# Loading q with its token blocks outermost in a fused attention and feed-forward kernel

## The chip, the cores and the metric

The kernel runs on one core of a Trainium2 chip. Its time is the device time of one execution in microseconds (us). The kernel before took 860.06 us in the median of three runs (860.0 to 861.02). Five engines work side by side, each through its own fixed list of instructions: TensorE (PE; its weight loads are shown apart as PEld), VectorE (DVE), ScalarE (ACT), GpSimd (POOL) and SyncE (SP), whose list here is nearly all DMA issues. The transfers themselves are carried out by 16 DMA engines.

## The reference

Three stages follow each other; shapes are q, k, v (4, 8, 576, 64) and phi (4, 8, 576, 32), all float32.

```python
a = exp(phi - max(phi, axis=2)); a = a / (sum(a, axis=2) + 1e-09)      # over the 576 tokens
k_m = einsum('bhsm,bhsd->bhmd', a, k); v_m = einsum('bhsm,bhsd->bhmd', a, v)   # 32 memory slots per head
scores = (q @ k_m^T) / sqrt(64); attn = softmax(scores, axis=-1)
x = (attn @ v_m) laid out as (4 * 576 tokens, 8 heads * 64)            # 2304 x 512
x = (h * sigmoid(h)) @ w_out,  h = x @ w_in                            # 512 -> 2048 -> 512
out = ((x @ w_a) * (x @ w_b)) @ w_out2                                 # 512 -> 1536 -> 512
```

## The kernel before

The program has three parts. The first one, some 125 us long, loads q, k, v, phi and the first weights and computes the attention of the four batches b = 0 to 3, and begins the first feed-forward stage on the batches that are ready. The second and third parts, the rest of the time, are the two feed-forward stages; they hold no work on q.

In the first part each batch goes through these steps. `weights(b)` (line 629) turns phi into exponentials on VectorE and ScalarE (tiles `m`, `mxa`, `mb`, `ex`). `memory(b)` (line 656) forms k_m and v_m on TensorE (tile `kvp`), scales them (`kvn`) and turns k_m (`kt`, `kT`); `values(b)` turns v_m (`vt`). `turn(b, hg, n)` (line 720) turns q. The eight heads are taken in two groups, hg = 0 and 1, with four heads x = 0 to 3 each. A tile `qq` holds one group of one batch: 128 partitions, each with J * D = 18 * 64 numbers, which is the stretch of 18 neighbouring tokens of one head; 32 such blocks i make up a head's 576 tokens. TensorE transposes 128 columns at a time (two tokens of 64 numbers) into a PSUM tile `qt`, three transposes for each n = 0, 1, 2; ScalarE copies `qt` to the tile `qT` in SBUF (line 731). A column of `qT` is a partition of `qq`. `scores(b, hg, p)` (line 751) takes 32 columns per head from `qT` (line 768), so the head is expected as the outer and the block as the inner index of a column. The softmax of the scores (tiles `x`, `mxq`, `smq`, `xt`, `at`) follows on VectorE and ScalarE. `vw_first` multiplies v_m into the weights (`mp`, `m0h`, `m0l`), and `mul_h` and `mul_y` are the feed-forward products (`hp`, `yp`).

All loads are issued by SP in one written order (`LOADS`, line 955): phi of b = 1 and 0, a piece of w_out, q of (b 0, hg 0), w_out, w_in, k and v of b = 0, two pieces of w_in, q of (0, 1), k and v of b = 1, q of (1, 1), w_out, q of (1, 0), (2, 0), (2, 1), phi of b = 2 and 3, w_in, k and v of b = 2, k and v of b = 3, w_out, q of (3, 0), (3, 1). An issue waits until the buffer that it fills is free: there are two for `qq`, two pairs for k and v, three staging tiles for weights. SP also keeps at most eight loads open: each load uses one of eight completion counters in turn and waits until the load that used it before has landed. The order of the instructions of every engine is set ahead of time by a planner (`run`, line 566) with fixed assumed durations (1500 ns for a load of q, 490 ns for a copy of `qt`); on the chip each engine runs its list in that order whatever the real durations are. The planner also puts products of a tile of ones (`ones`) between TensorE's instructions where it expects a wait.

Of the kernel before, what the change touches and what calls it, by code (L numbers as in the profile page):

```python
# [13 lines left out]
AF = mybir.ActivationFunctionType  # L14
# [6 lines left out]
def attn_moe_moe2_kernel(  # L21
# [59 lines left out]
    V, A, GP, T, Y = (Pinned(e) for e in (nc.vector, nc.scalar, nc.gpsimd, nc.tensor, nc.sync))  # L81
# [444 lines left out]
    def op(eng, ns, after=(), done=None, take=None, free=(), wait=100, table=None, rec=0):  # L526
        takes = [] if take is None else [take] if isinstance(take[0], str) else list(take)
        return eng, ns, after, done, takes, free, wait, table, rec
# [78 lines left out]
    def bank_of(kind, name):  # L607

        pool, tag = {"bank": (ps_t, "t"), "hp": (ff["h"], "hp"), "yp": (ff["y"], "yp")}[kind]
        ps = pool.tile([128, W], F32, tag=tag, name=name)  # L610
        keep_busy(ps)
        return ps
# [107 lines left out]
    def turn(b, hg, n):  # L720

        t = st[b]
        yield op("T", 650, [f"q{b}{hg}"] + [f"qT{b}{hg}"] * (n > 0), done=f"qT{b}{hg}" if n == 0 else None,
                 take=[(BANK_Q[b], f"qt{b}{hg}{n}")] + [("qT", f"qT{b}{hg}")] * (n == 0), rec=6)
        if n == 0:
            t["qT", hg] = p_s.tile([128, J // 2, 128], F32, tag="qT", bufs=2, name="qT")
        qt = bank_of(BANK_Q[b], "qt")[:, :384].rearrange("p (i s) -> p i s", i=3)
        for i in range(3):
            T.transpose(qt[:, i], t["qq", hg][:, 128 * (3 * n + i) : 128 * (3 * n + i) + 128], ident)
        yield op("A", 490, done=f"qt{b}{hg}{n}", free=[f"qt{b}{hg}{n}"] + [f"qq{b}{hg}"] * (n == 2))  # L730
        A.activation(out=t["qT", hg][:, 3 * n : 3 * n + 3], in_=qt, func=AF.Copy)

    def low_half(way, v_ns, a_ns, hi, lo, src, done, free):

# [108 lines left out]
    def loads():  # L843

        st["w"] = {}
        for what in LOADS:
            kind, b, hg = what[:-2].rstrip("0123456789"), int(what[-2]), int(what[-1])
            if kind == "phi":
                yield op("D", 1500, done=f"phi{b}", take=("ph", f"ph{b}"))
                ph = st[b]["ph"] = p_in.tile([128, 4, JP, NM], F32, tag="ph", name="ph")  # L850
                Y.dma_start(
                    out=ph.rearrange("p x c m -> p x (c m)"),
                    in_=phi[b].rearrange("(x r) (p c) m -> (r p) x (c m)", r=2, p=64),
                )
            elif kind == "kv":
                yield op("D", 3050, done=f"kv{b}{hg}", take=("kv", f"kv{b}{hg}"))
                kv = st[b]["kv", hg] = p_in.tile([128, 2, 2, JP * D], F32, tag="kv", name="kv")
                for i, s in enumerate((k, v)):
                    src = s[b, 4 * hg : 4 * hg + 4].rearrange("(x r) (p c) d -> (r p) x (c d)", r=2, p=64)
                    Y.dma_start(out=kv[:, i], in_=src)  # L860
            elif kind == "q":

                yield op("D", 1500, done=f"q{b}{hg}", take=("qq", f"qq{b}{hg}"))
                qq = st[b]["qq", hg] = p_in.tile([128, J * D], F32, tag="qq", bufs=2, name="qq")
                src = q[b].rearrange("(x g) (i j) d -> g x i (j d)", g=2, i=32)[hg]
                Y.dma_start(out=qq, in_=src)
            else:
                c = hg
                name = f"{kind}{c}"
                yield op("D", 1400, done=f"load_{name}", take=("st", f"st_{name}"))  # L870
                s64 = st["w"][name] = p_w.tile([128, W], U64, tag="st", bufs=3, name="st_" + name)
                if kind == "wi":

                    r0, c0 = 256 * (c % 2), 256 * (c // 2)
                    src = w_in[r0 : r0 + 256, c0 : c0 + 256].rearrange("(a p) n -> p a n", p=128)
                    Y.dma_start(out=s64.rearrange("p (a b) -> p a b", a=2), in_=src)
                else:
                    Y.dma_start(out=s64, in_=w_out[c * 128 : c * 128 + 128, :])
# [95 lines left out]
    free_at["T"] = 5400.0  # L974
    free_at["D"] = 1900.0
    add(0, loads())
    add(R["units"][0], feed_forward())
    for b in range(B):
        add(R["weights"][b], weights(b))
        add(R["memory"][b], memory(b))  # L980
        if SUMS[b] == "V":
            add(R["sums"][b], sums(b))
        add(R["values"][b], values(b))
        for hg in range(2):
            for n in range(3):
                add(R[f"turn{hg}"][b], turn(b, hg, n))
            for p in range(len(parts_of(b))):
                add(R[f"scores{hg}" if p == 0 else f"late{hg}"][b], scores(b, hg, p))
        if b == 0:
            add(R["first"][0], vw_first(0, (0,)))  # L990
            add(R["vw"][0], vw_first(0, (1,)))
        else:
            add(R["vw"][b], vw_first(b, (0, 1)))
# [39 lines left out]
    with ExitStack() as mctx:  # L1033
# [110 lines left out]
        def due_weights(n):  # L1144
            return 10 + (START + NP * NS * QUARTER * (n // WG) - 8000.0 - 22000.0 * (WG - 1 - n % WG)) / 1000
# [173 lines left out]
        for n in later:  # L1319
            t = due_weights(n)  # L1320
# [36 lines left out]
```

## Time and profile before

| what | value |
|---|---|
| median of three runs | 860.06 us (860.0 to 861.02) |
| the profiled execution, whole | 860.02 us |
| its span, first to last instruction | 858.2 us |
| PE busy in the span | 808.8 us, 94% |
| PE busy in the first 125 us | 82.23 us |
| PE busy from 125 to 160 us | 35.00 us of 35 |
| eight loads of q | 576 KB each, 128 pieces of 4608 bytes |

A row of the chain of waits names what the work that ended last was waiting for. A row of the timeline gives the start, the length, the engine, the operation with output and inputs, the number of instructions that it merges, and in brackets how long the engine had been idle and what ended that wait. In the windows, PEclk is the granted TensorE clock as a share of the full 2.4 GHz (0.50 is 1.2 GHz), and the DMA share is the mean busy share of the 16 DMA engines.

### The profile page before, as it was taken

The page shows a single profiled execution, that of the slowest core. Times are in us where ns is not written, and L with a number is a line of the kernel's source. Part 1 is how long each engine was busy: PE and PEld are TensorE (multiplying, and loading weights), DVE is VectorE, ACT ScalarE, POOL GpSimd, SP SyncE. Part 2 cuts the span into 40 slices and gives each one's busy share as a digit, 9 for nine tenths or more (in the row PEclk, how much of TensorE's full clock was granted, in tenths as well). Part 3 has the DMA queues.
Part 4 walks back from the last instruction along what each step waited for, and adds up shares of the span by engine and source line. Part 5 has one row for each costly group of instructions (what it writes and reads, how often), then busy time and mean ns, then how long its engine had stood idle before and what let it go on. Part 6 is the DMA issues. An engine that isn't in the chain of part 4 may idle for free.

```text
span 858.2 us, 14574 instructions
## 1 busy us (share of the span) xinstructions
PE 808.8 (94%) x5826; PEld 744.7 (87%) x5826; DVE 536.6 (63%) x1052; ACT 440.7 (51%) x891; POOL 56.9 (7%) x71
## 2 busy tenths in 40 slices
PE   4664889999999999999999999999999999999997
PEld 3453779979999999999989999999999999999996
DVE  3564678765664666666579887486764865634534
ACT  1534577876565446566646766635443553322220
POOL 0000000000000000022200111101010110100000
PEclk8778989999999999999999999999999999999999
DMA  9828620253222123254466969979775985656753
GB/s 236 224 101 212 197 77 1 75 146 76 75 62 62 50 75 99 43 121 102 87 242 249 289 193 284 286 227 278 223 215 185 274 241 169 185 179 202 199 157 75
DMA packets 58644, 138.84 MB, mean 162 GB/s; under 512 B 4944, under 2 KB 30032, under 8 KB 58576
## 3 DMA queue, kind: packets, MB, share of 16 engines
q1 hardware_dynamic: 48352, 122.44, 45.1%
q0 software_dynamic: 9072, 14.95, 10.3%
q8 instruction: 46, 0.75, 0.4%
q10 hardware_dynamic: 1152, 0.52, 0.3%
q14 instruction: 22, 0.18, 0.1%
HBM read 101.71 MB, written 21.23 MB: 143 GB/s over the span
## 4 chain that ended last, share of the span: by engine, by line
PE 86%; DMA 11%; DVE 1%; ACT 1%; SPq 1%; issue 0%
PE ab L69 30%; PE yp L69 23%; PE op L69 17%; PE hp L69 12%; DMA qq<-in_q_dram 10%; PE mp L69 2%; PE qt L69 1%; DMA st_b<-in_moe_w_b_dram 1%; SPq L69 1%; DVE yq L69 0%; PE sc L69 0%; PE kvp L69 0%; DVE T L69 0%; DVE ex L69 0%; ACT e_wo L69 0%
## 5 line engine op out<-in xcount | busy, mean ns | idle before, releaser
L69 PE MATMUL ab<-yq,wh 128*128 128x384 f32 x1080 | 260.3, 338 | 2.1 <-DVE yq L69 1.2
L69 PEld LDWEIGHTS ab<-yq,wh 128*128 128x128 f32 x1080 | 196.4, 189 | 9.3 <-DVE yq L69 1.5
L69 PE MATMUL ab<-yq,wl 128*128 128x384 f32 x432 | 145.9, 338 | 0.0
L69 ACT ACTIVATE u<-ab 128x384 f32<-128x384 f32 x108 | 52.5, 491 | 86.8 <-PE ab L69 86.3
L69 DVE TENSOR_TENSOR gl<-g,gh 128x288 fp32r<-128x288 f32 x128 | 58.1, 455 | 60.2 <-ACT gh L69 60.2
L69 ACT ACTIVATE g<-hp 128x288 f32<-128x288 f32 x128 | 52.1, 408 | 80.5 <-PE hp L69 71.9
L69 DVE TENSOR_TENSOR y<-op,y 128x512 f32<-128x512 f32 x54 | 37.3, 691 | 77.9 <-PE op L69 77.1
L69 PE MATMUL op<-wol,ph 128*128 128x512 f32 x216 | 85.4, 395 | 0.0
L69 PE MATMUL op<-woh,pl 128*128 128x512 f32 x216 | 85.1, 394 | 0.0
L69 PE MATMUL op<-woh,ph 128*128 128x512 f32 x216 | 84.3, 390 | 0.0
L69 PEld LDWEIGHTS ab<-yq,wl 128*128 128x128 f32 x432 | 81.6, 189 | 0.0
L69 DVE TENSOR_TENSOR u<-ab,u 128x384 f32<-128x384 f32 x108 | 59.8, 555 | 20.7 <-PE ab L69 19.7
L69 ACT ACTIVATE ph<-u 128x384 fp32r<-128x384 f32 x72 | 37.4, 524 | 66.9 <-DVE u L69 60.3
L69 DVE TENSOR_TENSOR y<-yp,y 128x288 f32<-128x288 f32 x104 | 47.3, 456 | 28.7 <-PE yp L69 28.5
L69 ACT ACTIVATE gh<-g 128x288 fp32r<-128x288 f32 x128 | 56.4, 443 | 3.1
L69 PEld LDWEIGHTS op<-woh,pl 128*128 128x128 f32 x216 | 40.5, 188 | 8.9
L69 PE MATMUL qt<-ident,qq 128*128 128x128 f32 x72 | 16.0, 372 | 33.1 <-DMA qq<-in_q_dram 32.5
L69 PEld LDWEIGHTS op<-woh,ph 128*128 128x128 f32 x216 | 40.6, 188 | 6.7
L69 PEld LDWEIGHTS op<-wol,ph 128*128 128x128 f32 x216 | 40.5, 187 | 6.7
L69 PEld LDWEIGHTS qt<-ident,qq 128*128 128x128 f32 x72 | 11.3, 189 | 38.1 <-issue 21.0
L69 PE MATMUL yp<-gh,wo_0h 128*128 128x288 f32 x128 | 38.7, 303 | 2.6 <-DVE ex L69 1.3
L69 DVE TENSOR_TENSOR pl<-u,ph 128x384 fp32r<-128x384 f32 x72 | 39.3, 552 | 2.0 <-ACT ph L69 1.8
(171 smaller groups left out, 1796.8 us busy)
## 6 DMA issues: line engine op xcount, KB each, us to landing
yq<-yd SPq DMA_DIRECT2D x63, 768.0 KB, 4.3
yd<-yq SPq DMA_DIRECT2D x21, 768.0 KB, 4.3
st_wo<-in_moe_w_out_dram SPq DMA_DIRECT2D x16, 512.0 KB, 3.7
st_wi<-in_moe_w_in_dram SPq DMA_DIRECT2D x16, 512.0 KB, 4.0
st_a<-in_moe_w_a_dram SPq DMA_DIRECT2D x12, 512.0 KB, 5.2
st_b<-in_moe_w_b_dram SPq DMA_DIRECT2D x12, 512.0 KB, 5.6
wl<-s POOLq DMA_DIRECT2D x24, 256.0 KB, 5.9
st_o<-in_moe_w_out_dram SPq DMA_DIRECT2D x12, 512.0 KB, 6.0
```

What stands on the lines that cost most here:

```text
L69: ins = f(*a, **k)
```

## The change

The source of a load of q is described to the DMA with three dimensions. Before, the outermost was the head x (4 rows far apart), then the block i (32), then 1152 contiguous numbers; now it is the block i (32), then the head x (4), then the same 1152 numbers. Partition p of `qq` held x = p // 32, i = p % 32 and now holds i = p // 4, x = p % 4. Each partition still receives 4608 contiguous bytes. ScalarE's copy reads `qt` with the head as the outer and the block as the inner index, a step of four numbers (16 bytes) from one element to the next, and writes `qT` without gaps in the order that it had before. Everything after `qT` is the same, and so is the order of the instructions on all five engines: no instruction is added, removed or moved.

```diff
-        A.activation(out=t["qT", hg][:, 3 * n : 3 * n + 3], in_=qt, func=AF.Copy)
+        A.activation(
+            out=t["qT", hg][:, 3 * n : 3 * n + 3].rearrange("p a (x i) -> p a x i", x=4),
+            in_=qt.rearrange("p a (i x) -> p a x i", x=4), func=AF.Copy,
+        )
...
-                src = q[b].rearrange("(x g) (i j) d -> g x i (j d)", g=2, i=32)[hg]
+                src = q[b].rearrange("(x g) (i j) d -> g i x (j d)", g=2, i=32)[hg]
                 Y.dma_start(out=qq, in_=src)
```

## Rows read from the trace of the kernel before

**Rows 1.** Windows: busy time by engine, PEclk, DMA share, GB/s.

```profile
core 0: us, PE busy (x) PEld busy (x) DVE busy (x) ACT busy (x) POOL busy (x), PEclk, DMA share, GB/s
0.00:125.00 125.00, 82.23 (x1240) 63.37 (x1241) 66.68 (x135) 56.23 (x114) 1.27 (x8) 0.82 0.65 180
125.00:858.00 733.00, 726.59 (x4588) 681.29 (x4586) 469.95 (x918) 384.47 (x778) 55.63 (x63) 1.00 0.55 159
```

**Rows 2.** Chain of waits from 0 to 128 us: start, length, what.

```profile
2.33 17.59 DMA qq<-in_q_dram
26.26 14.35 DMA qq<-in_q_dram
44.26 15.79 DMA qq<-in_q_dram
63.62 14.75 DMA qq<-in_q_dram
94.93 23.28 DMA qq<-in_q_dram
```

**Rows 3.** PE's waits from 0 to 126 us: total, times, longest.

```profile
PE qt L69 <- DMA qq<-in_q_dram: 32.5, 8, 10.0
PE kvp L69 <- DMA kv<-in_v_dram: 2.8, 2, 1.5
```

**Rows 4.** DMA traffic from 45 to 64 us.

```profile
DMA packets 431, 1.90 MB, mean 100 GB/s; under 512 B 14, under 2 KB 14, under 8 KB 428
q1 hardware_dynamic: 428, 1.86, 25.4%
```

**Rows 5.** DMA traffic from 7.5 to 20 us.

```profile
DMA packets 1015, 2.60 MB, mean 208 GB/s; under 512 B 54, under 2 KB 54, under 8 KB 1015
q1 hardware_dynamic: 1015, 2.60, 103.7%
```

**Rows 6.** DMA traffic from 40 to 42.5 us.

```profile
DMA packets 391, 0.98 MB, mean 394 GB/s; under 512 B 22, under 2 KB 22, under 8 KB 391
```

**Rows 7.** Timeline, TensorE at the turns of q and two products of k and v.

```profile
19.96 2.38 PE L69 MATMUL qt<-ident,qq 128*128 128x128 f32 x9 [9.97 <-DMA qq<-in_q_dram]
...
28.36 0.41 PE L69 MATMUL kvp<-kv,ex 64*32 64x128 f32 x6 [0.72 <-ACT e_wi L69]
...
40.74 0.88 PE L69 MATMUL qt<-ident,qq 128*128 128x128 f32 x3 [4.59 <-DMA qq<-in_q_dram]
...
47.19 1.07 PE L69 MATMUL kvp<-kv,ex 64*32 64x128 f32 x56 [1.23 <-DMA kv<-in_v_dram]
...
78.50 1.51 PE L69 MATMUL qt<-ident,qq 128*128 128x128 f32 x6 [8.74 <-DMA qq<-in_q_dram]
...
111.76 2.35 PE L69 MATMUL qt<-ident,qq 128*128 128x128 f32 x9 [3.04 <-DMA qq<-in_q_dram]
...
118.34 0.84 PE L69 MATMUL qt<-ident,qq 128*128 128x128 f32 x6 [0.18 <-DMA qq<-in_q_dram]
```

**Rows 8.** Timeline, VectorE at phi's arrivals and ScalarE before q's turn.

```profile
5.04 0.56 DVE L69 TENSOR_TENSOR m<-ph 128x384 f32<-128x384 f32 x1 [5.04 <-DMA ph<-in_phi_dram]
...
71.42 0.44 ACT L69 ACTIVATE gh<-g 128x288 fp32r<-128x288 f32 x1
...
79.76 0.56 DVE L69 TENSOR_TENSOR m<-ph 128x384 f32<-128x384 f32 x1 [9.04 <-DMA ph<-in_phi_dram]
```

**Rows 9.** Windows around turns of q, clock low and high.

```profile
111.70:115.30 3.60, 3.54 (x15) 3.23 (x16) 1.45 (x3) 2.58 (x7) 0.00 (x0) 0.50 0.37 129
118.30:121.00 2.70, 2.66 (x21) 2.56 (x21) 2.08 (x5) 2.54 (x7) 0.00 (x0) 1.00 0.17 71
```

**Rows 10.** ScalarE's groups from 0 to 126 us: busy, mean ns, idle before.

```profile
L69 ACT ACTIVATE qT<-qt 128x384 f32<-128x384 f32 x24 | 11.4, 491 | 38.5 <-PE qt L69 38.0
...
L69 ACT ACTIVATE e_wo<-st_wo 128x512 f32<-128x512 f32 (+1 forms) x8 | 5.3, 665 | 10.1 <-DMA st_wo<-in_moe_w_out_dram 10.1
...
L69 ACT ACTIVATE wo_1h<-t_wo 128x512 fp32r<-128x512 f32 x1 | 0.6, 618 | 0.0
```

## The prediction

> **What bounds the kernel now.** I read the windows first. From 125 us to the end TensorE is busy 726.59 of 733 us at a granted clock of 1.00; nothing there touches q, so this part will follow whatever happens before it, at the same length. In the first 125 us TensorE is busy for only 82.23 us, so 42.8 us are idle, at a mean clock of 0.82 [rows 1]. All that can be won by better loading lies in these 42.8 us, and in the low clock beside them.
>
> The chain of waits says what the idle time is for. Up to 128 us its five longest pieces are all loads of q, 14.35 to 23.28 us each from issue to landing [rows 2]. TensorE's own waits agree: 32.5 us in eight waits end with a load of q, and only 2.8 us with a load of v [rows 3]. A wait for data is a wait for time only if the data could come sooner, so the next view is the DMA traffic. From 45 to 64 us hardly anything but q is in flight, and it moves 100 GB/s with 25.4% of the 16 engines busy: a quarter of them, that is four, which is the size of the outermost dimension of the source of q [rows 4]. The other loads, whose source has its 128 partitions outermost, reach 394 GB/s [rows 6]. Where q and other loads are in flight together the sum is 208 GB/s, and the share reads full [rows 5]; the others lose half their rate as well. I read this as four engines that carry q and their part of everything else, with the rest held to their pace; the rows do not name single engines, so that is a reading and not a measurement.
>
> The Trainium skill has this rule (DMA: Bandwidth & Descriptors, "Why a DMA increments its semaphore by 16 and not by 1"): the number of engines of a transfer is the largest up to 16 that divides the slowest dimension, larger than one, of both its sides. By it the old source (4) and tile (128) give four engines, and the new source (32) gives 16; the trace agrees for four, and no row here shows 32.
>
> **The change, part by part.** No instruction is added, removed or moved, so there are two costs: how long a load of q takes, and how long a copy takes.
>
> *Loads.* 0.59 MB at 394 GB/s take 1.5 us; at 100 GB/s they take 5.9. For what a load takes besides its bytes I use the first load of phi: it landed 5.04 us after the span's start [rows 8], less 1.5 us for the same 0.59 MB leaves 3.5 us, the issue included. A load of q on an empty path should then land at most 5.0 us after its issue, against 14.35 us or more today. That the new order reaches 394 GB/s is an estimate from the other loads; the lower bound of the rate is the mixed 208 GB/s, 2.8 us a load. I take 394, because q alone runs each quarter of the engines at a quarter of 394 already, with the same pieces of 4608 bytes.
>
> Now I follow TensorE's waits in order [rows 7] and ask of each what is late next.
>
> First turn (19.96, after 9.97 of waiting). Ahead of this q lie two phi and one piece of weights; with q that is 2.29 MB, 5.8 us at 394, plus 3.5: landed at 9.3. TensorE comes at 9.99. The whole wait goes: 9.97.
>
> Next the product of k and v of b = 0, at 28.36. Its list up to the last of these k and v is 5.70 MB: 14.5 + 3.5 = 18.0, and it is wanted at 28.36 - 9.97 = 18.4. Just in time.
>
> Second q (40.74, after 4.59). Its issue at 26.26 [rows 2] hangs on staging tiles that ScalarE frees after the first turn, so it moves along to 16.3; the 7.34 MB up to it are through at 18.6 + 3.5 = 22.1. TensorE comes at 36.15 - 9.97 = 26.2. The 4.59 go; total 14.56.
>
> From 40.74 to 78.50 TensorE waits 1.23 for v, which shares the path with q and lands earlier, then in all 5.98 for three loads of q (32.5 less the other five waits), then 8.74 for (2, 1). That last load is issued at 63.62, when the tile before it has been turned; TensorE comes for it at 69.76, 6.1 us later, and the load takes 5.0. So these waits go too: 1.23 + 5.98 + 8.74 = 15.95. But now something else is late. ScalarE ends its last piece ahead of this turn's copies at 71.86, 2.1 us after TensorE's 69.76 [rows 8], and the third transpose group and the next products wait for its copies. VectorE had been free since 70.72 and waited for phi until 79.76 [rows 8]; phi stands right behind q in SP's list and needs (0.59 + 1.18) MB, 4.5 + 3.5 = 8.0 us from 63.62 on, 0.9 after VectorE. Both delays lie beside each other; I charge 2.1.
>
> From 78.50 to 125, 3.04 and 0.18 go. The other wait for v, 1.5 [rows 3], stays: k and v of b = 3 are issued when TensorE frees their tiles, with no q in front of them. The clock also pays: after the wait of 3.04 the next 15 matrix products run at 0.50, 3.54 us of busy time, where 21 of a similar mix take 2.66 at 1.00 [rows 9]. That is 0.236 against 0.127 us, and 15 times the difference is 1.6 us. Elsewhere the clock may stay low, since TensorE still stops between pieces; I count nothing there.
>
> *Copies.* All 24 take 491 ns now [rows 10]. Reading in steps of 16 bytes out of PSUM occurs nowhere in the trace. The nearest row is a read in steps of 8 bytes out of SBUF: 665 ns for 512 numbers against 618 without gaps [rows 10], 47 ns more. It can't gain, since the number of elements is the same. For the upper bound I take twice today's time, 24 * 0.49 = 11.8 us, if all of it were on the path. I take the nearest row, 24 * 0.035 = 0.8 us in all (47 ns scaled to 384 numbers), of which at most a quarter, 0.2 us, lies where ScalarE is late.
>
> Here the skill speaks against the change (Advanced Engine Details and Errata, "PSUM Cachelines"): PSUM is read in lines of two float32 numbers and "every two consecutive elements should be contiguous for best throughput". By it each number would need a line of its own, and the copies would cost up to the 11.8 us of the upper bound; no row here shows it.
>
> *Sum.* 32.5 (q) + 1.2 (v) + 1.6 (clock) - 2.1 (ScalarE) - 0.2 (copies) = 33.0. The profiled execution took 860.02 us, 858.2 of it span; less 33.0 is 827.0. The median, 860.06, is the same within 0.04.
>
> **Rivals.**
>
> 1. *Sixteen engines, but still half rate beside other loads.* For it: the mixed 208 GB/s is not explained by any row. Against it: q alone and the others alone both run at the full rate for their engines. After the first 1.7 MB the 4.0 MB up to k and v of b = 0 would take 19.2 us instead of 10.2, 9 us late at the first product; k, v and q of b = 1 lose a like amount but overlap the work between, some 4 more. Time: 827 + 13 = 840.
>
> 2. *The load stays on four engines.* If the split were decided by something other than the order of the source, nothing is won, and the copies cost 0 to 11.8: 860 to 872. Against it: 25.4% busy matches a dimension of four.
>
> 3. *Slower: ScalarE's copy takes over.* ScalarE runs its list in order, and a transpose group waits for the copy of an earlier one. From 33.0 / 24 = 1.4 us more a copy, 1.9 us in place of 0.49, the gain is eaten up. At 2.0 us more, 24 * 2.0 = 48 less 33 gives 875. Against it: ScalarE is busy 56.23 of the first 125 us [rows 1], and no copy in the rows is slower than 1.3 ns a number; this needs 5.
>
> 4. *More is won.* If the whole 42.8 us of idle time went, the time would be 817. It can't quite, as the first 5 us wait for phi.
>
> **How the numbers follow.** My forecast has a chance of 0.84, with a range of its own of 818 to 834 (ScalarE's lateness doubled or gone, the clock's share between 0 and 6 us, the copies up to 5 on the path). Rival 1 gets 0.08, rival 2 0.04 (three parts in four within 0.2%, the rest slower), rival 3 0.02, rival 4 0.02. The range for 8 in 10 is 816 to 840. About 0.2%, 1.7 us, is what a measurement of this kernel can tell from no change. Faster: 0.84 + 0.08 + 0.02 = 0.94; same 0.03; slower 0.03.
>
> **What would show it.** In the profile after, the 576 KB of a load of q should pass in about 1.5 us with the DMA share near full, no stretch should stay at 0.25, and no piece of the chain of waits before 125 us should be a load of q of over 10 us. TensorE's waits for q should fall from 32.5 to under 3 us. New waits should be on ScalarE or VectorE around the turn of q of (2, 1), some 30 us earlier than now. `qT` should read 0.49 to 0.55 us; near 0.98 speaks for the skill's line rule. A DMA rate of 208 GB/s beside q means rival 1. I am wrong at the root if the DMA share stays at a quarter while q alone is in flight, or if the part after 125 us changes its length.

## The result, and the profile after

The changed kernel takes 828.07 us in the median of four runs (824.87 to 830.38), against 860.1 us (860.0 to 861.02) for the kernel before on the same chip. The ratio is 0.9623, with a 95% interval of 0.9584 to 0.9661. The forecast was 827.0 us. The execution with the profile below is the longest of the four, 830.38 us with a span of 828.6, so it shows 29.6 us of the gain where the median shows 32.0. The others have spans of 824.5, 828.0 and 823.1; the mean granted clock is 0.992 in the two short ones and 0.984 and 0.983 in the two long ones.

First the windows, as in [rows 1]. The first part now ends at 95 us: the first product with `m1h`, which stood at 125.32 us, stands at 95.77. The columns are those of [rows 1].

```profile
0.00:95.00 95.00, 79.99 (x1237) 60.48 (x1238) 66.18 (x134) 56.02 (x114) 1.28 (x8) 0.87 0.67 236
95.00:828.00 733.00, 725.56 (x4591) 680.24 (x4590) 470.43 (x918) 384.96 (x778) 55.75 (x63) 1.00 0.54 159
```

The second part has kept its length: from the first product with `m1h` to the end of the span it is 732.9 us before and 732.8 after. In the first, TensorE's idle time has gone from 42.8 to 15.0 us, and its busy time, for the same work, from 82.23 to 79.99: the clock rose from 0.82 to 0.87. That is 27.8 and 2.2 of the 30 us by which the window is shorter.

The DMA traffic from 7.5 to 20 us answers to [rows 5], the stretch in which q and other loads are in flight together:

```profile
DMA packets 2151, 4.93 MB, mean 394 GB/s; under 512 B 134, under 2 KB 134, under 8 KB 2151
...
q1 hardware_dynamic: 2151, 4.93, 104.8%
```

At the same full share the 16 engines move 394 GB/s in place of 208. The load of q of (2, 1), which has an almost empty path, shows it from issue to landing. This is the list of DMA issues from 47 to 53 us; the last number is the median us to landing, where the chain before had 14.75 for this load [rows 2]:

```profile
qq<-in_q_dram SPq DMA_DIRECT2D x1, 576.0 KB, 4.3
```

TensorE's waits from 0 to 95 us (total, times, longest) answer to [rows 3]. No wait ends with q, and 0.4 us are left of the 2.8 for v. The waits for `qT` make 2.3 us; 1.2 of them, at `yp`, stood in the kernel before too:

```profile
PE kvp L69 <- issue: 3.3, 1, 3.3
PE kvp L69 <- ACT wo_2h L69: 1.7, 1, 1.7
PE qt L69 <- issue: 1.6, 2, 1.2
...
PE yp L69 <- ACT qT L69: 1.2, 1, 1.2
PE qt L69 <- ACT qT L69: 1.1, 3, 0.6
...
PE kvp L69 <- DMA kv<-in_v_dram: 0.4, 1, 0.4
```

The longest wait left was not forecast: 3.3 us that end with "issue", that is, in which TensorE waited for nothing that the profile shows. The timeline of TensorE, at the places of [rows 7], shows where it stands:

```profile
9.60 0.82 PE L69 MATMUL qt<-ident,qq 128*128 128x128 f32 x6
...
18.17 2.31 PE L69 MATMUL kvp<-kv,ex 64*32 64x128 f32 x144 [1.74 <-ACT wo_2h L69]
20.41 0.27 PE L69 MATMUL kvp<-ones,ex 64*128 64x1 f32 x1
23.95 3.62 PE L69 MATMUL kvp<-ones,ex 64*128 64x1 f32 x35 [3.27 <-issue]
...
29.53 0.90 PE L69 MATMUL qt<-ident,qq 128*128 128x128 f32 x3
...
52.53 0.87 PE L69 MATMUL qt<-ident,qq 128*128 128x128 f32 x6
...
57.02 0.40 PE L69 MATMUL yp<-gh,wo_0h 128*128 128x288 f32 x1 [1.18 <-ACT qT L69]
...
82.41 1.24 PE L69 MATMUL qt<-ident,qq 128*128 128x128 f32 x5
84.01 1.12 PE L69 MATMUL qt<-ident,qq 128*128 128x128 f32 x4 [0.36 <-issue]
...
88.63 0.87 PE L69 MATMUL qt<-ident,qq 128*128 128x128 f32 x6
```

No turn of q waits for its load any more. The stop is in the middle of the sums of the first batch's weights (`kvp<-ones,ex`): one product runs, then nothing for 3.27 us. The kernel before has a shorter stop at the same product:

```profile
31.94 2.17 PE L69 MATMUL kvp<-ones,ex 64*128 64x1 f32 x35 [1.07 <-issue]
```

The windows, in the changed kernel, of the stop and of what follows:

```profile
20.60:24.00 3.40, 0.13 (x3) 0.05 (x2) 0.45 (x2) 0.67 (x1) 0.00 (x0) 1.00 0.96 297
24.00:27.60 3.60, 3.57 (x35) 3.48 (x35) 0.16 (x1) 0.00 (x0) 0.00 (x0) 0.56 1.04 401
```

The granted clock is near its lower level (0.56, where 0.50 is 1.2 GHz) after the stop, and the 35 products take 3.57 us, where they took 2.17 before. So the stop costs twice, 3.27 us and then 1.4.

ScalarE's copy, the other half of the change, is as it was; the timeline groups of `qT` give a minimum, median and maximum of 472, 491 and 526 ns where it had a mean of 491 [rows 10]:

```profile
L69 ACT ACTIVATE qT<-qt x24: 472/491/526, 10.1 to 90.8; 128x384 f32<-128x384 f32 x24
```

### The profile page after: what moved, and what is told of

It reads as the page before. It is cut to its first block, busy times and chain, and to the rows that moved or that the text cites. A ratio compares the mean times of both kernels' runs of the same rounds, so it can differ in the third digit from the quotient of the medians.

```text
span 828.6 us, 14574 instructions
## 1 busy us (share of the span) xinstructions
PE 805.6 (97%) x5826; PEld 740.7 (89%) x5826; DVE 536.6 (65%) x1052; ACT 441.0 (53%) x891; POOL 57.0 (7%) x71
## 3 DMA queue, kind: packets, MB, share of 16 engines
q10 hardware_dynamic: 1152, 0.52, 0.3%
## 4 chain that ended last, share of the span: by engine, by line
PE 93%; DMA 3%; DVE 2%; issue 1%; ACT 1%; SPq 0%; ACTq 0%
PE ab L69 31%; PE yp L69 25%; PE op L69 18%; PE hp L69 12%; PE kvp L69 2%; PE mp L69 2%; DMA kv<-in_v_dram 1%; PE qt L69 1%; PE sc L69 1%; DMA st_b<-in_moe_w_b_dram 1%; DMA ph<-in_phi_dram 1%; DVE yq L69 0%; PE kt L69 0%; DVE t_wo L69 0%; DVE m L69 0%
## 5 line engine op out<-in xcount | busy, mean ns | idle before, releaser
L69 PE MATMUL yp<-gl,wo_0h 128*128 128x288 f32 x128 | 38.1, 298 | 0.0
L69 PE MATMUL yp<-gh,wo_1h 128*128 128x288 f32 x128 | 38.0, 297 | 0.0
```

Of the source, the lines that this page charges most:

```text
L69: ins = f(*a, **k)
```

## The experiments

The kernel before took 861.06 us (858.85 to 864.32) beside e1, e3, e4 and e7, 861.17 (858.44 to 864.63) beside e0, e5, e6 and e8, and 860.57 (858.42 to 866.29) beside e9 and e10. All ratios are to it.

**e1: the copy alone.** The kernel before with ScalarE's read in steps of four numbers. The load keeps its old order, so the heads reach `scores` in another order than the reference's.

```diff
+        A.activation(out=t["qT", hg][:, 3 * n : 3 * n + 3].rearrange("p a (x i) -> p a x i", x=4),
+                     in_=qt.rearrange("p a (i x) -> p a x i", x=4), func=AF.Copy)
...
                 src = q[b].rearrange("(x g) (i j) d -> g x i (j d)", g=2, i=32)[hg]
```

> The kernel before with only ScalarE's new copy: it reads the turned q in steps of 16 bytes. The load keeps the old order, so the heads of q come out in a wrong order and the output is not the reference's. Theory (the gain is all in the load, the copy costs nothing): qT stays at 0.49 us, DMA share at 0.25 while q alone is in flight, time 860 within 1.7 us. Rival (a read in steps costs up to twice): qT near 0.98 us, 24 times 0.49 us, time 862 to 872.

It took 860.81 us (858.2 to 864.42), ratio 0.9993 [0.9975, 1.0012]. The DMA traffic from 45 to 64 us is that of [rows 4], 100 GB/s at a share of 25.1%. The copy took, as minimum, median and maximum:

```profile
L69 ACT ACTIVATE qT<-qt x24: 473/491/525, 20.5 to 121.2; 128x384 f32<-128x384 f32 x24
```

So all of the gain is the load's, and this copy costs nothing more when it reads PSUM in steps of 16 bytes: 491 ns with and without them. The rule of the Trainium skill (Advanced Engine Details and Errata, "PSUM Cachelines") that every two consecutive elements should be contiguous for best throughput does not show in this copy.

**e7, e4 and e3: the outermost number of the source.** These three split a load of q into parts, so that the outermost dimension is 2, 8 or 32. e7 keeps the old order and copy and loads two heads at a time; e4 has the new order and copy and loads eight blocks at a time; e3 keeps the old order and copy and loads one head at a time, whose 32 blocks are then outermost.

```diff
+ for x in range(2): Y.dma_start(out=qq[64 * x : 64 * x + 64], in_=src[2 * x : 2 * x + 2])     # e7
+ for x in range(4): Y.dma_start(out=qq[32 * x : 32 * x + 32], in_=src[8 * x : 8 * x + 8])     # e4
+ for x in range(4): Y.dma_start(out=qq[32 * x : 32 * x + 32], in_=src[x])                     # e3
```

> The kernel before, old order and old copy, but each load of q issued as two loads of two heads each: 2 is outermost. Theory (engines): both loads share the same two engines, DMA share near 0.125 and about 50 GB/s while q alone is in flight; the two engines carry 4.72/2 + 16.3/16 = 3.38 MB, 1.18 MB more than the four of before, which at 24.6 GB/s for an engine is 48 us: 890 to 925. Rival (order is the cause): as before, 860 within 3. Another rival (two loads take different engines): 860 as well, at a share of 0.25.

> The changed kernel, new order and new copy, but each load of q issued as four loads of 8 blocks by 4 heads: 8 is outermost. Theory (engines): eight engines, a DMA share near 0.5 and about 200 GB/s while q alone is in flight. The busiest engines carry 4.72/8 + 16.3/16 = 1.61 MB of the first part, between 2.20 MB with four engines and 1.31 MB with sixteen, so of the 32 us about a third is lost: 830 to 842. Rival (order is the cause): as the changed kernel, 828 within 3, and 390 GB/s.

> The kernel before, old order of partitions and old copy, but each load of q issued as four loads, one head each, with the 32 blocks outermost. Theory (the number of DMA engines that the outermost dimension allows is the cause): 32 outermost spreads each over all engines, no stretch at a DMA share of 0.25, TensorE waits for q under 3 us, time 826 to 836 (24 more issues of about 0.5 us on SP). Rival (the order of the addresses or of the partitions written is the cause): as before, 860, with 100 GB/s while q alone is in flight.

e7 took 899.39 us, ratio 1.0439 [1.041, 1.0467]; e4 834.86, 0.9675 [0.9638, 0.9713]; e3 833.45, 0.9676 [0.965, 0.9703]. First a window of e7 from 60 to 65 us in which hardly anything but q is in flight, then the DMA traffic of e4 from 33 to 37 us, the same:

```profile
60.00:65.00 5.00, 0.00 (x0) 0.00 (x0) 0.94 (x2) 0.00 (x0) 0.00 (x0) 0.67 0.13 52
```

```profile
DMA packets 231, 0.87 MB, mean 216 GB/s; under 512 B 38, under 2 KB 38, under 8 KB 230
...
q1 hardware_dynamic: 230, 0.85, 52.4%
```

While q is alone, the share of the 16 engines goes with the outermost number: 0.13 and 52 GB/s at 2, 0.25 and 100 at 4 [rows 4], 0.52 and 216 at 8. At 32, the changed kernel from 34.4 to 36.8 us, it is 0.79 and not full:

```profile
DMA packets 144, 0.59 MB, mean 246 GB/s; under 512 B 16, under 2 KB 16, under 8 KB 144
...
q1 hardware_dynamic: 144, 0.59, 79.2%
```

The next load, alone from 42.0 to 44.5 us, has 236 GB/s. The trace's records of single pieces (start, length, size) tell why, and give the number. The commonest number of q's pieces in flight at one time is 2 in e7, 4 before, 8 in e4 and 16 in the changed kernel; so these are 2, 4, 8 and 16 engines. The first sixteen pieces of the load at 34.4 us take 211 to 852 ns each, where its median piece takes 178: it starts slowly. With the old order and the old copy e3 wins most of the gain, so it is the number and not the order of the partitions. TensorE's waits for q were 68.1 us in e7, 32.5 before, 6.1 in e4, 1.2 in e3 and none in the changed kernel.

Why does e3, on 16 engines, stay some 5 us behind? Its windows while the first loads land show a full share all along and, once q is in flight (from 6.7 us), less than the full rate:

```profile
4.00:7.00 3.00, 2.59 (x23) 1.76 (x21) 1.95 (x5) 0.00 (x0) 0.00 (x0) 1.00 1.07 387
7.00:10.00 3.00, 2.05 (x9) 0.75 (x7) 2.80 (x8) 0.97 (x2) 0.00 (x0) 1.00 1.06 256
```

In the trace's records the pieces of the first q take 301 ns in the mean there, against 182 in the changed kernel; by load the means are 240 to 307 ns against 179 to 253. In e3 up to 16 pieces at once go into the same 32 partitions, and come from one stretch of 144 KB; no run tells which of the two slows them. TensorE's waits for "issue" before `kvp` are 5.9 us in place of 3.3, for q 1.2 in place of none, for v 1.0 for 0.4. But the profiled execution is the shortest of e3's five (span 828.8 us): its idle time in the first 95 us is 17.5 us against 15.0, and the clock, 0.89 against 0.87, gives that back. So the slower pieces are shown, and that they make up the 5 us between the medians is not.

**e0 and e5: the stop of 3.3 us.** e0 is the changed kernel again. e5 leaves out the planner's filling products of ones (not the sums `kvp<-ones,ex`), so TensorE has fewer instructions.

```diff
-        for _ in range(spare[0]):
+        for _ in range(0):
```

> The changed kernel once more, beside the next three on the same chip, since its first four runs spread over 5.5 us (824.9 to 830.4) in step with the granted clock (0.992 and 0.984). Expected 825 to 831, two groups; no theory is at stake.

> The changed kernel without the products of ones that the planner puts between TensorE's instructions; all other instructions keep their order. In the changed kernel TensorE then stands still for 3.3 us after the first product of kvp with ones, put down to issue, with the DMA engines full and a 16 KB piece of instructions starting only inside this wait. Theory (TensorE waits for its next piece of instructions, which queues behind loads): the list is 60 instructions shorter up to there, so the wait moves some 30 products on, to the end of the 36 products with ones or behind them, and stays 1 to 5 us long. Rival (something fixed at that product holds it): the wait stays behind the first product with ones. For the time: the products of ones fill 4.6 us before the first product of k and v, which waits for data anyway, so 826 to 831; if their only use is to keep the clock up, later products at 0.50 cost 2 to 6 us: 830 to 836.

e0 took 827.01 us (825.03 to 829.42), ratio 0.9602 [0.9576, 0.9627], with the same stop of 3.27 us, ended at 23.89. e5 took 825.74 (822.7 to 826.72), 0.958 [0.9557, 0.9603]: the intervals overlap. TensorE's timeline in e5:

```profile
18.03 4.12 PE L69 MATMUL kvp<-kv,ex 64*32 64x128 f32 x144 [3.86 <-DMA kv<-in_v_dram]
22.08 2.18 PE L69 MATMUL kvp<-ones,ex 64*128 64x1 f32 x36
...
26.19 0.90 PE L69 MATMUL qt<-ident,qq 128*128 128x128 f32 x3
...
60.08 0.62 PE L69 MATMUL kvp<-kv,ex 64*32 64x128 f32 x18 [1.63 <-issue]
```

The stop is gone from this place, and the second q is turned at 26.19, the 26.2 of the prediction. That they meet is in part luck, since the idle time where the filling products were leaves the clock low (0.52 from 18.0 to 22.1 us) and the 144 products took 4.12 us instead of 2.31, while the stop of 1.07 us that the prediction's 26.2 still held is gone. A stop of 1.6 us for "issue" now stands at the products of b = 2. I had expected the stop to move some 30 products on; it went further, so that part of the expectation failed. That the stop depends on how many instructions TensorE has passed is shown. What ends it can be read from the traces. The DMA traffic of the changed kernel from 20.5 to 24 us (first below) holds a 16 KB piece of instructions, in flight from 21.62 to 22.72 us; the stop ends at 23.95. The kernel before has such a piece from 28 to 36 us (second below), in flight from 29.56 to 30.58, and its stop ends at 31.94. Over all traces, 23 of the 24 stops of TensorE for "issue" that last over 0.3 us end 1.2 to 1.8 us after such a piece has landed. That TensorE waits there for instructions is the reading that fits; it is a reading of times, and no run delayed a piece by itself.

```profile
q1 hardware_dynamic: 390, 1.02, 93.3%
q8 instruction: 1, 0.02, 2.0%
```

```profile
q1 hardware_dynamic: 646, 1.58, 74.9%
q8 instruction: 1, 0.02, 0.8%
```

Why the piece comes so late stays open. At this place the stop is long where the loads fill the engines around the piece (93.3% and 3.27 us after, 100.0% and 4.8 us in e3) and short where they don't (74.9% and 1.07 us before, 64.0% and 1.3 us in e4), as if the piece waited among the loads. But e5's stop of 1.63 us speaks against that as the whole cause: its piece starts at 57.45 us, after 1.9 us in which no DMA engine is busy (55.5 to 57.4). No experiment took the loads away and kept the instructions.

**e6 and e8: who is late at the turn of (2, 1).** Both issue phi of b = 2 and 3 ahead of q of (2, 1), e8 also k and v of b = 2. The order of all other engines is kept.

```diff
+                load_phi(2); load_phi(3)                      # e6 and e8, before the load of q of (2, 1)
+                load_kv(2, 0); load_kv(2, 1)                  # e8 alone
```

> The changed kernel with the two loads of phi of b = 2 and 3 issued ahead of q of (2, 1); the instructions of the four other engines keep their order. VectorE waits 5.0 us for phi at 56 in the changed kernel, because SP holds phi back until TensorE has turned q of (1, 0). Theory (this is what is late next, not ScalarE as the prediction had it): VectorE's wait goes, TensorE reaches the product yp at 57.0 some 1 to 3 us sooner, and the time falls by 1 to 3 us to 823 to 828, unless k and v of b = 2, which land at 63.2, become what is waited for. Rival (ScalarE sets the pace there): phi lands early, and TensorE's time at yp stays within 0.5 us; time unchanged.

> The changed kernel with phi of b = 2 and 3 and k and v of b = 2 issued ahead of q of (2, 1); the instructions of the four other engines keep their order. The DMA engines are idle from 31 to 47 us but for q, so these loads land before they are wanted. Theory (loads held back in SP's list are what is late next): no wait for phi or for v of b = 2, TensorE's first product of k and v of b = 2 (62.5 us) 2 to 4 us sooner, time 822 to 827. Rival (ScalarE and VectorE set the pace from 50 to 62 us): less than 1 us sooner than with phi alone.

The expectation of e6 took a wait of 5.0 us for phi as standing here. It is the first phi's, at the start [rows 8]; at the turn of (2, 1) VectorE takes phi up at 53.48 us without a wait. e6 took 826.07 us (825.78 to 826.62), ratio 0.959 [0.9568, 0.9611], no different from e0. From the turn to the first `yp` it is 4.49 us, as in the changed kernel (52.53 to 57.02):

```profile
50.52 0.88 PE L69 MATMUL qt<-ident,qq 128*128 128x128 f32 x6
...
55.01 0.41 PE L69 MATMUL yp<-gh,wo_0h 128*128 128x288 f32 x1 [1.19 <-ACT qT L69]
```

So phi's arrival does not set the pace. e8 took 832.99 (830.62 to 834.59), 0.9669 [0.9647, 0.9692], 6 us more than e0, which neither its theory nor its rival had: q is issued at 45.78 us behind 3.5 MB, and TensorE waits for it again. Whether earlier k and v alone would gain anything it does not tell.

```profile
56.57 1.51 PE L69 MATMUL qt<-ident,qq 128*128 128x128 f32 x6 [6.33 <-DMA qq<-in_q_dram]
```

**e9 and e10: the two small edits together, and less work for ScalarE.** e9 is e6 without the filling products. e10 replaces the silu by a plain copy (it leaves out the silu), which takes away nine of ten table loads of 1.28 us.

```diff
-        A.activation(out=g32, in_=hp, func=AF.Silu)
+        A.activation(out=g32, in_=hp, func=AF.Copy)
```

> The changed kernel with both small edits that seemed to gain 1 us each: phi of b = 2 and 3 issued ahead of q of (2, 1), and no products of ones between TensorE's instructions. Theory (each edit takes away a separate stop: the stop of 3.3 us in the first part, and none for phi): if both were real gains they add, 825.0 us. Rival (differences of 1 us between these kernels are the spread of their runs, which goes with the mean granted clock, and the clock takes back what the missing products save): 825.7 to 827, its interval overlapping that of the changed kernel's second run, 827.0 (825.0 to 829.4). A third possibility: without the products of ones the clock is low for longer, and phi ahead of q makes q of (2, 1) late: over 828.

> The changed kernel with the silu between the first and second feed-forward product replaced by a plain copy on ScalarE (this leaves out the silu; the number of instructions and their sizes stay), so that ScalarE never has to load another function table. Theory (between the turn of q of (2, 1) and the next products TensorE waits for ScalarE, whose stretch there is a table load of 1.28 us, four activations and two copies): the interval from the start of that turn to the first yp product, 4.49 us in four traces, falls to about 3.2 us, with no other wait in its place. In all ten table loads of 1.28 us go; those on the path are worth 1 to 4 us of the time, so 823 to 826 us. Rival (something else, VectorE's ex or the transposes themselves, holds this interval): it stays above 4.2 us and the time is 827 as before.

e9 took 827.48 us (824.84 to 827.7), ratio 0.9594 [0.9566, 0.9622]: the edits don't add, and neither is a gain that these runs can tell from none. TensorE waits 4.5 us for v in its profile, in the place where the filling products stood. e10 took 827.03 (826.05 to 828.07), 0.96 [0.957, 0.963], as e0, and my theory for it fell. The interval is 4.48 us still. ScalarE's timeline first in the changed kernel, then in e10:

```profile
51.74 1.28 ACT L69 ACT_TABLE_LOAD   x1
53.03 0.41 ACT L69 ACTIVATE g<-hp 128x288 f32<-128x288 f32 x1
...
54.60 0.86 ACT L69 ACTIVATE qT<-qt 128x384 f32<-128x384 f32 x2
55.71 0.41 ACT L69 ACTIVATE g<-hp 128x288 f32<-128x288 f32 x1 [0.25 <-PE qt L69]
```

```profile
51.46 0.85 ACT L69 ACTIVATE qT<-qt 128x384 f32<-128x384 f32 x2
53.98 0.41 ACT L69 ACTIVATE g<-hp 128x288 f32<-128x288 f32 x1 [1.67 <-PE mxt L69]
```

The table load is gone, and ScalarE idles for 1.67 us in its place. VectorE and TensorE in e10 say why:

```profile
50.98 0.85 DVE L69 STREAM_TRANSPOSE x<-sc 128x288 f32<-128x288 f32 x2 [0.25 <-PE sc L69]
51.75 0.52 DVE L69 TENSOR_TENSOR m<-ph 128x384 f32<-128x384 f32 x1
...
53.22 0.29 DVE L69 TENSOR_TENSOR mxa<-mxa,m 128x128 f32<-128x128 f32 x1
```

```profile
50.81 0.88 PE L69 MATMUL qt<-ident,qq 128*128 128x128 f32 x6
52.32 0.49 PE L69 MATMUL qt<-ident,qq 128*128 128x128 f32 x3
53.66 0.30 PE L69 MATMUL mxt<-ident,mxa 128*128 128x128 f32 x1 [0.85 <-DVE mxa L69]
55.29 0.40 PE L69 MATMUL yp<-gh,wo_0h 128*128 128x288 f32 x1 [1.33 <-ACT qT L69]
```

`mxt` stands ahead of the products in TensorE's list and needs VectorE's maximum, whose chain starts when the scores are ready and runs without a gap. It ends so that `mxt` starts 2.85 us after the turn; in the changed kernel, where ScalarE's copies let TensorE come to it, 2.99 (52.53 to 55.52). The two chains end within 0.14 us of each other, so taking away one is worth nothing here. No variant beat the changed kernel beyond the spread of its runs.

## Why the prediction was right, step by step

The place-by-place account, as the shift of each place to the left, against the profiled run:

| place | before us | after us | shift | forecast |
|---|---|---|---|---|
| first turn of q | 19.96 | 9.60 | 10.4 | 10.0 |
| products of k and v, b = 0 | 28.36 | 18.17 | 10.2 | 10.0 |
| second q | 40.74 | 29.53 | 11.2 | 14.6 |
| q of (2, 1) | 78.50 | 52.53 | 26.0 | 30.5 |
| first `yp` after it | 83.34 | 57.02 | 26.3 | 28.4 |
| q of (3, 0) | 111.76 | 82.41 | 29.4 | 31.5 |
| q of (3, 1) | 118.34 | 88.63 | 29.7 | 33.2 |
| span | 858.2 | 828.6 | 29.6 | 33.0 |

The forecast column is the running sum of the prediction's terms; the clock's 1.6 is counted at (3, 1), the 0.2 for the copies in the last row.

- *Loads on all engines, 32.5 us.* The waits are right: nothing is left of the 32.5. The rate is right beside other loads (394 GB/s) and too high for q alone, 246 and 236 where I had 394. The load at (2, 1) still lands in 4.3 us where I had set at most 5.0: in the records its pieces pass in 2.6 us and not 1.5, which leaves 1.7 us for the rest and not 3.5. Two wrong terms cancel there. Rivals 1 and 2 are out by these rows, and rival 4 by the 15.0 us of idle time that are left. e1, e4 and e7 show the mechanism: the outermost number of the source sets how many engines work. This is the rule of the Trainium skill that the prediction named (DMA: Bandwidth & Descriptors, "Why a DMA increments its semaphore by 16 and not by 1"); four values, 2, 4, 8 and 32, now agree with it. All four are powers of two, so no run here tests its words on divisors.
- *Waits for v, 1.2.* Better than forecast: 2.4 went, since the second wait, which I had kept at 1.5, shrank as well.
- *No new wait in the first stretch.* Wrong, and this is the step that cost most. The working followed data and buffers only; the "issue" stop, 1.07 us before, grew to 3.27, that is by 2.2, and the low clock after it took 1.4 more: 3.6 us, against the 3.4 by which the second q is late. "Just in time" at 18.4 us held (18.17).
- *TensorE's arrival at (2, 1).* It lost 1.1 us more on the forecast, by another stop for "issue" of 1.21 us at 40.09: a second case of the same failed step.
- *ScalarE late at (2, 1), -2.1.* Right in kind and too dear. ScalarE is late by what I had: its copies start at 54.60, 2.1 us after the turn. But from the turn to the first `yp` it is 4.49 us, where the charge made 4.84 + 2.1. These are the windows of that stretch, before and after:

```profile
78.50:83.34 4.84, 3.61 (x17) 3.35 (x17) 3.45 (x8) 2.27 (x6) 0.00 (x0) 0.66 0.81 292
52.53:57.02 4.49, 2.65 (x24) 1.92 (x16) 4.17 (x10) 4.14 (x11) 0.00 (x0) 1.00 1.07 381
```

TensorE's idle time grew by 0.6 us only (1.23 to 1.84), because the stretch before already held a wait for `qT`. And its busy time fell by 1.0, since the clock was 1.00 and not 0.66: a gain that I had counted at nothing. e10 corrects the reason too: without ScalarE's table load the stretch is as long, because VectorE's maximum ends with ScalarE's copies. I had VectorE only waiting for phi, which it did not; charging once for both was right.
- *Clock, 1.6.* In size about right, in place wrong, so the size is luck. Busy time fell by 2.2 us in the first part, but at the turn of (3, 0) the clock is low again: 0.50 from 82.41 to 85.20 us, though no wait stands before it and TensorE was busy for all of the 5.4 us up to it at 1.00. There 4 transposes start behind another stop of 0.36 us and take 1.12, so (3, 0) to (3, 1) won 0.4 of the 1.8 that I had put there. The gain came elsewhere, 1.0 of it at (2, 1).
- *Copies, 0.2.* Zero, by e1. Rival 3 is out.
- *The part after 125 us.* The same 733 us.

By the profiled run the sum of 33.0 is 3.4 too high. That this is the size of the first stop is chance: the misses are -3.4 up to the second q, -1.1 more up to (2, 1), +2.4 at `yp` and -1.4 on the clock from (3, 0) to (3, 1), and some of them cancel. The median, 828.07, is 1.1 above the forecast, and the second set of five runs, 827.01, falls on it; the runs of one kernel spread by some 5 us, in step with the mean clock, so a match this close is luck. The mechanism, the waits for q that went and the unchanged second part are not.

## What to carry to other kernels

Look at the share of DMA engines while a suspect load is alone: a share of a quarter or an eighth, at a matching rate, points to a source whose outermost dimension is too small, and the same bytes described with 32 in front took 3.8% off this kernel. When loads stop being the bound, sum the waits that remain by their releaser, "issue" among them: here one such stop grew to three times its length for a cause that stays open. And where one engine sets the pace, read when the others' chains into the same instruction end, before taking anything away from it.

## What the runs showed that I had not expected

- A load on four engines slows those beside it: from 7.5 to 20 us the path moves 208 GB/s against 394 at a share of 1.04, and in the records a 2304-byte piece of k or v takes 191 ns in the median against 98. So its price is more than its own length.
- Pieces of 4608 bytes that go 16 at a time from one stretch of 144 KB into one group of 32 partitions take 301 ns in the mean, where pieces spread over 128 partitions take 182 (the first q in e3 and in the changed kernel).
- TensorE's stop for "issue" at one place went from 1.07 us (before) to 3.27 (after) and 4.8 (e3), without any change in its instructions. These stops end 1.2 to 1.8 us after a 16 KB piece of instructions has landed.
- Nine table loads of 1.28 us on ScalarE, taken away, changed the time by no more than its spread (827.03 and 827.01 us): the one at (2, 1) stood on one of two chains of equal length.
